# A recurrent attention and gated MLP kernel: the written order of its first part replaced on all engines

## The chip, the cores and the metric

The kernel runs on one core of one Trainium2 chip. The metric is the device time of one execution in microseconds (us); the time of a kernel is the median of its runs. A core has TensorE (PE; its weight loads are shown as PEld), VectorE (DVE), ScalarE (ACT), GpSimd (POOL) and SyncE (SP, which here only issues DMAs). Each engine works through its own queue in order and waits at semaphores for the others.

## The reference

A linear recurrence over 768 time steps for 4 batches and 8 heads of 48 channels, then a gated MLP over all 3072 tokens (model width 384, hidden width 1536). Everything is float32.

```python
for t in range(S):                                   # attention, per batch b and head h
    cur = einsum('bhd,bhe->bhde', u[None] * kt, vt)
    y[:, :, t] = einsum('bhd,bhde->bhe', rt, state + cur)
    state = w[None, :, :, None] * state + einsum('bhd,bhe->bhde', kt, vt)
...
gate = 1.0 / (1.0 + np.exp(-(x @ w_gate)))           # x: y as (tokens, 384)
val = x @ w_val
return (gate * val @ w_out).astype(np.float32)
```

## The kernel before

**The tiling.** Time is cut into 12 chunks of 64 steps, the heads into two halves; a chunk with a half is a *group*, and n counts the 24 groups (`GROUPS`, L34: half 1 of a chunk comes ahead of half 0). A group computes the 64x64 scores of keys and queries, applies them to the values, adds what the state gives, and updates the state. Two chunks (512 token columns, four groups) make one *tile* of x for the MLP; there are six. The MLP of a tile runs over 12 slices f of the hidden width, which the kernel calls items. Every operand of the MLP is split into a high part that the fast float32 mode holds exactly and a low rest, and a product is three passes (`PASS`, L499): 9 matmuls for the gate, 9 for the value (`up`, L507), 9 for the output (`down`, L546). x, the hidden activations and the weights are all split on the chip.

**What sets the order.** All engines run in the order in which the program is written (`manual_schedule`, L89). From tile 1 on, a loop (L674) writes it: gate and value of an item, at four items of the tile one group of attention, then the output of the item before. The first part, groups 0 to 7, all of tile 0 but its last `down`, and the first steps of groups 8 and 9, is written out by hand as a list of steps in `START` (L43), run by L650. It also holds all weight preparation. The change lies in this list and in the functions that its steps call.

**The steps**, with the engine that runs them (n is a group, f a weight slice; an item i of the old list stands for slice f and columns):
- SP: `L.n` loads queries and keys by channel (L100, tile `chan`, 3 buffers), `X.n` keys and values by token (L105, `toks`, 3 buffers), `Y.n` queries by token (L110), `W.f` one weight slice (L229, 1152 KB; f = 0 in two halves), `F.n` six DMAs that move parts of x between partitions (L480, L487).
- Preparing a group: `A.n` bonus keys (ACT, four instructions, L283), `R.n` queries (POOL; `Rv.n` on DVE, L291), `k.n` keys (DVE, L302), `T.n` token keys (POOL; `Tv.n` on DVE, L306).
- Attention on PE: `Z.n` scores (L366, two blocks of 32 small matmuls up to n = 7, into the one tile `sc`), `I.n` apply (L389, a block, and from n = 2 on a block more for the state, L347), `O.n` outer products (L407, a block). Behind them `K.n` copies the scores under masks (DVE, two instructions, L380), `d.n` decays the state (ACT, L424), `s.n` adds to it (DVE; `sa.n` on ACT, L435), `h.n` and `l.n` write the high and low part of x (ACT and DVE, L472, L476; two instructions, four for n = 1 and n = 3).
- A weight slice: `c.f` casts the upper words (ACT, L235), `j.f` joins the words (DVE, L242), `w.f` rounds to the high part (ACT, L251), `o.f` takes the low rest (POOL; `ov.f` on DVE, L257). A suffix 0 is a half of slice 0.
- The MLP: `U.i` gate and value (PE, 18 matmuls), `g.i` sigmoid (ACT, L522), `m.i` product (DVE, L527), `H.i` high part (ACT, L531), `q.i` low part (POOL; `qv.i` on DVE, L536), `D.i` output (PE, 9 matmuls). Items 0 and 1 are slices 0 and 1 on the first 256 columns (groups 0 and 1), items 2 and 3 the same slices on the other 256 (groups 2 and 3), items 4 to 13 slices 2 to 11 on all 512.
- Tables: `tc` constants, `tk`, `ti`, `tp`, `tr`, `tt`, `tn` powers of the decay in several layouts.

**PSUM.** `sc` takes two banks, `ring` (L71) has three banks, shared by the outputs of a group (two) and the gates and values of an item (one each), and `acc0` to `acc2` hold the output sums.

## Time and profile before

| | |
|---|---|
| median of 3 runs | 530.65 us (530.6 to 532.59) |
| span of the profiled execution | 532.9 us |
| PE busy | 510.4 us (96%) |
| PEld, DVE, ACT, POOL busy | 424.4, 203.4, 186.9, 189.9 us |
| DMA | 47.84 MB, mean 90 GB/s |

The span of the profiled execution lies 2.25 us over the median and inside 0.4 us of the slowest of the three runs. Busy time counts an engine's instructions without the semaphore and branch work between them; a matmul's end is modelled, so a busy PE need not be a PE at full pace. The pace of PE is read from the starts of matmuls of one shape.

### The profile page before, as it was taken

To read this page: it belongs to the slowest core of one execution; us is meant where nothing else is said; L and a number is where in the kernel's file an instruction comes from. 1 tells how busy PE (TensorE), PEld (TensorE's weight loads), DVE (VectorE), ACT (ScalarE), POOL (GpSimd) and SP (SyncE) were. 2 spreads that over 40 slices of the span, in tenths; PEclk is the share of its full clock that TensorE was granted. 3 is DMA by queue.
4 is the path that set the end of the run, shared out by engine and by line. 5 is a ranking of instruction groups with operands and counts; after the bars stand their busy time and mean duration, and the time that the engine had idled before them with its cause. 6 is when DMAs were issued, how large, how long until landed. Compare 5 with 4: busy or idle time off the path is not lost. (4 is left out here: it accounts for less than half of the span.)

```text
span 532.9 us, 11951 instructions
## 1 busy us (share of the span) xinstructions
PE 510.4 (96%) x5204; PEld 424.4 (80%) x5204; DVE 203.4 (38%) x344; ACT 186.9 (35%) x396; POOL 189.9 (36%) x159
## 2 busy tenths in 40 slices
...
GB/s 321 366 111 352 301 112 284 4 103 21 127 87 26 71 106 1 145 86 17 80 61 48 145 87 0 97 34 72 146 17 2 11 11 10 60 0 1 0 2 64
DMA packets 15723, 47.84 MB, mean 90 GB/s; under 512 B 2384, under 2 KB 5200, under 8 KB 14256
## 3 DMA queue, kind: packets, MB, share of 16 engines
...
q8 instruction: 43, 0.70, 0.6%
q14 instruction: 16, 0.13, 0.1%
...
## 5 line engine op out<-in xcount | busy, mean ns | idle before, releaser
L516 PE MATMUL ring<-xt,wx 128*128 128x512 f32 (+1 forms) x1332 | 309.9, 387 | 0.9 <-ACT sg L525 0.5
L516 PEld LDWEIGHTS ring<-xt,wx 128*128 128x128 f32 x1332 | 247.8, 191 | 51.3 <-ACT sg L525 0.7
L538 POOL TENSOR_TENSOR h<-sg,h 128x512 fp32r<-128x512 f32 (+1 forms) x66 | 88.5, 1340 | 259.5 <-ACT h L534 259.5
L554 PE MATMUL acc<-h,wx 128*128 128x512 f32 (+1 forms) x666 | 161.6, 388 | 0.4 <-POOLq L714 0.4
L554 PEld LDWEIGHTS acc<-h,wx 128*128 128x128 f32 x666 | 121.2, 188 | 25.6 <-POOLq L714 0.8
L529 DVE TENSOR_TENSOR sg<-ring,sg 128x512 f32<-128x512 f32 (+1 forms) x74 | 50.0, 676 | 237.0 <-PE ring L516 235.6
L525 ACT ACTIVATE sg<-ring 128x512 f32<-128x512 f32 (+1 forms) x74 | 43.4, 586 | 157.4 <-PE ring L516 157.4
L534 ACT CAST h<-sg 128x512 fp32r<-128x512 f32 (+1 forms) x74 | 45.0, 608 | 144.2 <-DVE sg L529 138.2
L293 POOL TENSOR_TENSOR dec<-chan,tabk 128x512 f32<-128x512 f32 x21 | 29.0, 1381 | 12.5 <-PE ring L337 12.4
L478 DVE TENSOR_TENSOR xt<-ring,xt 112x256 fp32r<-112x256 f32 (+1 forms) x52 | 19.9, 418 | 33.1 <-ACT xt L474 33.0
L308 POOL TENSOR_TENSOR toks<-toks,tabn 128x384 f32<-128x384 f32 x19 | 24.0, 1267 | 13.7 <-DMA toks<-in_tk 13.7
L314 POOL TENSOR_TENSOR dec<-dec,toks 128x384 f32<-128x384 f32 x16 | 16.3, 1020 | 27.3 <-DMA dec<-in_rt 27.3
L304 DVE TENSOR_TENSOR chan<-chan,tabk 128x512 f32<-128x512 f32 x24 | 25.0, 1042 | 0.9 <-ACT dec L287 0.9
L375 PE MATMUL sc<-dec,chan 48*64 48x64 f32 x768 | 17.4, 231 | 7.7 <-DVE chan L304 7.6
L383 DVE COPY_PREDICATED score<-masks,sc 128x512 f32<-128x512 int32 x32 | 23.9, 747 | 1.9 <-PE sc L375 1.1
L428 ACT ACTIVATE state<-state,pw 112x96 f32<-112x96 f32 x80 | 23.4, 362 | 2.6 <-PE ring L337 2.6
L337 PE MATMUL ring<-score,toks 64*48 64x64 f32 (+1 forms) x768 | 17.2, 230 | 5.0 <-DVE score L383 4.1
L447 DVE TENSOR_TENSOR state<-state,ring 48x192 f32<-48x192 f32 (+1 forms) x52 | 17.9, 350 | 9.7 <-ACT xt L474 4.7
L375 PEld LDWEIGHTS sc<-dec,chan 48*64 48x64 f32 x768 | 15.0, 145 | 8.1 <-POOL dec L293 7.6
L247 DVE SCALAR_TENSOR_TENSOR wf<-wr,top 128x1152 int32<-128x1152 int32 (+1 forms) x13 | 16.9, 1310 | 9.4 <-ACT top L240 5.7
L337 PEld LDWEIGHTS ring<-score,toks 64*48 64x48 f32 (+1 forms) x768 | 14.6, 137 | 6.4 <-DVE score L383 4.8
L474 ACT CAST xt<-ring 112x256 fp32r<-112x256 f32 (+1 forms) x52 | 16.7, 364 | 7.6 <-PE ring L337 7.3
...
## 6 DMA issues: line engine op xcount, KB each, us to landing
...
xt<-xt SPq DMA_DIRECT2D x12, 32.0 KB, 4.2
```

What stands on the lines that cost most here:

```text
L293: eng.tensor_tensor(v4(t[:, 0]), v4(chan[n][:, 0]), bc2(table_of(n)[:, :, ::-1]), ALU.mult)
L304: nc.vector.tensor_tensor(v4(k), v4(k), bc2(table_of(n)), ALU.mult)
L308: eng.tensor_tensor(v4(k), v4(k), bc2(tabn[:, 4 * g : 4 * g + 4]), ALU.mult)
L337: nc.tensor.matmul(yb[n][bank][64 * half : 64 * half + m, cs], lhsT, rhs, start=first, stop=stop, skip_group_check=True,)
L375: nc.tensor.matmul(sc[64 * gm : 64 * gm + 64, be, o : o + C], kk[row, cs : cs + C], rr[row, cs : cs + C], start=True, stop=True,)
L383: nc.vector.copy_predicated(t.rearrange("q (b m i) -> q b m i", b=2, m=4), masks[:, m].bitcast(I32).unsqueeze(1).unsqueeze(1).broadcast_to ...
L516: nc.tensor.matmul(o[:, self.cols], w[a][:, g * DM + kt * P : g * DM + (kt + 1) * P], self.x[:, kt, b, self.cols], start=(k == 0), stop=(k ...
L525: nc.scalar.activation(sg[:, c], self.pair[f][0][:, c], AF.Sigmoid, scale=UP)
L529: nc.vector.tensor_tensor(sg[:, c], self.pair.pop(f)[1][:, c], sg[:, c], ALU.mult)
L534: nc.scalar.copy(out=h[:, 0, c], in_=sg[:, c])
L538: eng.tensor_tensor(h[:, 1, c], self.sg.pop(f)[:, c], h[:, 0, c], ALU.subtract)
L554: nc.tensor.matmul(self.acc[d][:, self.cols], w[a][:, 2 * DM + d * P : 2 * DM + (d + 1) * P], h[:, b, self.cols], start=(f == 0 and k == 0 ...
```

## The change

- `START` is a new list. In the new one, loads go `L.0 X.0 L.1 W.0 L.2 L.3 X.1 W.1 X.2` (before: `L.0 W.0 L.1 X.0 W.1 L.2 X.1 X.2 W.2`), and the weight slices are used in the order 0, 1, 6, 7, 8, 4, 9, 10, 3, 5, 11, 2 for the gate.
- `U` is parted into `u` (gate, 9 matmuls) and `v` (value, 9 matmuls), each with a `ring` bank of its own taken when it is written. Items are named by slice, with a and b for the two column halves of slices 0 and 1.
- On PE the new list puts `Z.0` to `Z.3`, `I.0` to `I.2` and `O.0` to `O.2` ahead of the first gate; the old one had `Z.0` to `Z.2`, `I.0`, `I.1`, `O.0` and `O.1` there. 14 matmuls of the identity (`N.14`) stand ahead of `Z.0`.
- Other engines: seven `k` go from DVE to POOL (`kp`), two `A` from ACT to POOL (`Ap`), three `w` and two `h` from ACT to DVE (`wv`, `hv`), the order table from DVE to ACT (`trA`), one `s` to ACT; of the ten `R` five instead of three are on DVE, of the ten `T` one instead of three; fewer `o` and `q` are on DVE. The constants are cut into steps of their own.
- Group 1 writes its outputs to `acc1` and `acc2` instead of two `ring` banks.
- The loop from tile 1 on is the same; only the way in which it names items differs.

```diff
@@ -41,19 +41,20 @@
 
 
 START = """
-L.0 W.0 L.1 X.0 W.1 L.2 X.1 X.2 tc A.0 tk ti.1 R.0 ti.0 k.0 tp tr Z.0 tt K.0 I.0 c0.0 A.1 c0.1 tn
-h.0 c.1 T.2 T.1 k.1 Rv.1 j0.1 l.0 Tv.0 j0.0 Z.1 O.0 W.2 F.0 W.3 L.3 L.4 W.4 X.3 j.1 K.1 I.1 O.1 A.2
-w0.0 sa.0 w.1 h.1 w0.1 o0.1 o.1 R.3 Rv.2 k.2 o0v.0 l.1 s.1 Z.2 K.2 U.0 I.2 O.2 g.0 c.2 d.2 A.3 m.0
-U.1 H.0 g.1 h.2 j.2 k.3 s.2 l.2 q.0 T.3 m.1 F.2 L.5 W.8 X.4 L.6 W.5 W.6 L.7 X.5 F.1 X.6 L.8 W.7 Z.3
-K.3 I.3 O.3 w.2 A.4 k.4 H.1 c.3 h.3 l.3 R.4 D.0 Z.4 U.2 d.3 s.3 g.2 c.4 j.3 w.3 j.4 qv.1 m.2 o.2
-U.4 H.2 g.4 w.4 A.5 K.4 q.2 U.3 D.2 g.3 Rv.5 m.3 k.5 ov.3 m.4 T.4 I.4 O.4 Z.5 H.3 A.6 d.4 h.4 H.4
-c.6 c.5 k.6 s.4 K.5 l.4 Tv.5 j.6 R.6 q.3 D.1 D.3 U.5 I.5 g.5 h.5 j.5 qv.4 l.5 m.5 o.4 Z.6 D.4 R.7
-O.5 U.6 A.7 d.5 H.5 K.6 k.7 s.5 q.5 T.6 w.5 ov.5 U.7 c.8 c.7 g.6 j.7 m.6 L.9 X.8 ub Y.8 W.9 W.10
-X.7 I.6 Z.7 O.6 D.5 w.6 g.7 ov.6 d.6 w.7 H.6 s.6 j.8 qv.6 h.6 l.6 m.7 w.8 ov.7 H.7 qv.7 D.6 U.8 K.7
-R.8 c.9 ov.8 g.8 m.8 Tv.7 H.8 U.9 qv.8 g.9 k.8 j.9 w.9 o.9 m.9 D.7 U.10 g.10 H.9 c.10 j.10 m.10 q.9
-D.8 I.7 H.10 d.7 Z.8 O.7 h.7 w.10 D.9 s.7 U.11 ov.10 l.7 W.11 F.5 X.9 F.6 F.3 F.7 F.4 Y.9 qv.10
-g.11 c.11 j.11 D.10 U.12 m.11 w.11 R.9 ov.11 U.13 g.12 H.11 qv.11 m.12 H.12 qv.12 g.13 t.8 D.11 b.8
-i.8 D.12 K.8 k.9 m.13 H.13 q.13 b.9 T.9 t.9 i.9 T.8
+L.0 tov.0 ta tk tz ts.0 ts.1 ti.1 tc A.0 tp tb to.1 k.0 X.0 N.14 L.1 trA ti.0 R.0 A.1 Z.0 R.1 K.0
+W.0 tt I.0 tn Tv.0 c0.0 kp.1 L.2 L.3 c0.1 j0.0 X.1 Z.1 h.0 l.0 w0.0 A.2 O.0 K.1 I.1 R.2 k.2 W.1 X.2
+o0.0 Z.2 F.0 j0.1 T.1 R.3 A.3 h.1 kp.3 sa.0 w0.1 c.1 K.2 O.1 l.1 j.1 T.2 I.2 h.2 d.2 Z.3 w.1 O.2 l.2
+s.2 X.3 u.0a L.4 K.3 g.0a sa.1 W.6 o0.1 v.0a W.7 o.1 m.0a A.4 F.2 I.3 H.0a qv.0a Rv.4 kp.4 u.1a h.3
+D.0a l.3 g.1a c.6 T.3 L.5 v.1a Z.4 d.3 O.3 m.1a j.6 H.1a s.3 c.7 u.0b u.1b wv.6 v.1b A.5 g.0b v.0b
+W.9 qv.1a D.1a W.8 g.1b j.7 w.7 L.7 ov.6 c.8 m.1b m.0b H.1b o.7 u.6 q.1b u.7 H.0b K.4 g.6 j.8 qv.0b
+g.7 W.4 wv.8 v.7 c.4 X.4 ov.8 v.6 D.0b j.4 R.5 m.6 W.5 u.8 H.6 kp.5 D.1b q.6 m.7 T.4 w.4 H.7 W.11
+X.7 g.8 I.4 L.6 W.10 c.9 Z.5 ov.4 O.4 u.4 X.5 d.4 q.7 ub Rv.6 j.9 s.4 g.4 Ap.6 D.7 v.8 hv.4 l.4 K.5
+w.9 X.6 c.10 m.8 L.8 H.8 T.5 v.4 I.5 kp.6 Z.6 q.8 ov.9 Ap.7 d.5 m.4 O.5 u.9 W.3 j.10 D.8 s.5 hv.5
+w.10 c.3 l.5 K.6 j.3 kp.7 o.10 c.5 v.9 wv.3 W.2 u.10 j.5 H.4 c.2 g.9 Rv.7 D.6 qv.4 g.10 o.3 m.9 c.11
+j.11 H.9 v.10 m.10 w.5 T.6 ov.5 u.3 q.9 j.2 L.9 X.9 w.11 o.11 g.3 I.6 Z.7 d.6 O.6 s.6 T.7 u.5 h.6
+kp.8 D.4 l.6 H.10 Rv.8 qv.10 K.7 Y.8 v.3 m.3 g.5 u.11 I.7 Z.8 O.7 F.6 w.2 h.7 ov.2 d.7 l.7 X.8 F.7
+Y.9 Rv.9 D.9 k.9 s.7 D.10 u.2 H.3 q.3 g.2 v.5 b.8 v.2 m.5 b.9 H.5 D.3 i.8 T.9 i.9 m.2 H.2 T.8 qv.5
+t.8 t.9 g.11 v.11 m.11 D.5 K.8 q.2 H.11 D.2 q.11
 """
...
+    def bonus_keys_on(n, eng):
+        t, k, g = dec_of(n), chan[n][:, 1], GROUPS[n][1]
+        eng.tensor_tensor(
+            t[:, 1].rearrange("q (m x) -> q m x", m=4), k.rearrange("q (m x) -> q m x", m=4),
+            wu[:, 1, 4 * g : 4 * g + 4].unsqueeze(2).broadcast_to([P, 4, 2 * C]), ALU.mult,
+        )
...
     def outputs(n):
-        yb[n] = one_bank(), one_bank()
+        if n == 1:
+            yb[n] = tuple(pacc.tile([P, 512], F32, name=f"acc{i}") for i in (1, 2))
+        else:
+            yb[n] = one_bank(), one_bank()
...
+        def up_one(self, f, g):
+            w, o, k = (whi[f], wlo[f]), one_bank(), 0
+            self.pair.setdefault(f, []).append(o)
+            for kt in range(3):
+                for a, b in PASS:
+                    nc.tensor.matmul(
+                        o[:, self.cols], w[a][:, g * DM + kt * P : g * DM + (kt + 1) * P],
+                        self.x[:, kt, b, self.cols], start=(k == 0), stop=(k == 8),
+                    )
+                    k += 1
+
         def up(self, f):
...
+            self.up_one(f, 0)
+            self.up_one(f, 1)
...
     steps = {
+        "ta": identity, "tb": causal_masks, "tc": first_table,
+        "ts": clear_scores, "tz": lambda: clear_state(), "to": clear_top, "tov": lambda i: clear_top(i, V),
...
         "N": idle_matmuls,
+        "A": bonus_keys, "Ap": lambda n: bonus_keys_on(n, G),
+        "k": keys, "kp": lambda n: keys(n, G),
+        "h": x_high, "hv": lambda n: x_high(n, V.tensor_copy),
+        "wv": lambda f: round_weights(f, ALL, V.tensor_copy),
...
+    moe_steps = {
+        "U": Moe.up, "u": lambda m, f: m.up_one(f, 0), "v": lambda m, f: m.up_one(f, 1), "g": Moe.sigmoid, "m": Moe.product, "H": Moe.h_high, "q": Moe.h_low,
+        "qv": lambda m, f: m.h_low(f, nc.vector),
     }
...
-    for i in range(n0, len(items)):
+    for i in range(1, len(items)):
...
-        if i == n0 + 8:
+        if i == 9:
```

The function behind `N`, which both kernels have and only the new list calls:

```python
    def idle_matmuls(k):
        t = pacc.tile([P, 512], F32, name="acc2")
        for _ in range(k):
            nc.tensor.matmul(t[:, 0:P], ident, ident, start=True, stop=True)
```

## Rows read from the trace of the kernel before

**Rows 1.** The page, busy time of each engine over the whole span

```profile
PE 510.4 (96%) x5204; PEld 424.4 (80%) x5204; DVE 203.4 (38%) x344; ACT 186.9 (35%) x396; POOL 189.9 (36%) x159
```

**Rows 2.** Busy time by stage: stretch, length, busy us (instructions), granted clock, DMA share, GB/s

```profile
0.00:41.38 41.38, 26.91 (x690) 24.25 (x690) 30.68 (x55) 24.83 (x57) 19.57 (x26) 1.00 0.70 262
41.38:121.81 80.43, 79.23 (x938) 66.17 (x933) 54.69 (x76) 47.85 (x87) 22.80 (x15) 1.00 0.50 189
121.81:532.90 411.09, 404.30 (x3584) 333.97 (x3582) 118.07 (x214) 114.25 (x253) 147.53 (x119) 1.00 0.17 53
```

**Rows 3.** Waits of PE, 0 to 41.38 us: us in total, times, longest

```profile
PE sc L375 <- DVE chan L304: 7.6, 1, 7.6
PE ring L337 <- DVE score L383: 4.1, 3, 2.2
```

**Rows 4.** Longest wait of PE in 41.38 to 121.81 us, then behind 121.81 us

```profile
PE ring L337 <- issue: 0.3, 2, 0.2
...
PE acc L554 <- POOLq L714: 0.4, 1, 0.4
```

**Rows 5.** Timeline of PE in the first part: start us, busy us, instructions

```profile
7.63 1.13 PE L375 MATMUL sc<-dec,chan 48*64 48x64 f32 x32 [7.63 <-DVE chan L304]
...
24.18 3.78 PE L516 MATMUL ring<-xt,wx 128*128 128x256 f32 x16 [0.18 <-DVE xt L478]
...
33.89 1.33 PE L516 MATMUL ring<-xt,wx 128*128 128x256 f32 x9 [0.47 <-ACT sg L525]
35.15 0.69 PE L375 MATMUL sc<-dec,chan 48*64 48x64 f32 x32
35.67 0.65 PE L375 MATMUL sc<-chan,dec 48*64 48x64 f32 x32
...
41.38 8.89 PE L516 MATMUL ring<-xt,wx 128*128 128x256 f32 x54
...
121.81 4.24 PE L516 MATMUL ring<-xt,wx 128*128 128x512 f32 x18
```

**Rows 6.** DVE groups by form, 0 to 122 us: xcount | busy us, mean ns

```profile
L247 DVE SCALAR_TENSOR_TENSOR wf<-wr,top 128x1152 int32<-128x1152 int32 x11 | 15.4, 1411 | 9.4 <-ACT top L240 5.7 <-issue 3.5
L383 DVE COPY_PREDICATED score<-masks,sc 128x512 f32<-128x512 int32 x17 | 12.6, 744 | 1.4 <-PE sc L375 1.1
L304 DVE TENSOR_TENSOR chan<-chan,tabk 128x512 f32<-128x512 f32 x10 | 9.3, 927 | 0.9 <-ACT dec L287 0.9
L478 DVE TENSOR_TENSOR xt<-ring,xt 112x256 fp32r<-112x256 f32 x12 | 4.5, 414 | 0.0
L478 DVE TENSOR_TENSOR xt<-ring,xt 48x256 fp32r<-48x256 f32 x8 | 3.4, 422 | 2.7 <-ACT xt L474 2.6
L447 DVE TENSOR_TENSOR state<-state,ring 112x192 f32<-112x192 f32 x10 | 3.2, 349 | 9.1 <-ACT xt L474 4.7 <-PE ring L337 4.3
```

**Rows 7.** DVE timeline: the first low part of x

```profile
13.02 0.75 DVE L478 TENSOR_TENSOR xt<-ring,xt 112x256 fp32r<-112x256 f32 x2
```

**Rows 8.** POOL groups by form, 0 to 122 us, as in rows 6

```profile
L293 POOL TENSOR_TENSOR dec<-chan,tabk 128x512 f32<-128x512 f32 x7 | 11.0, 1566 | 12.5 <-PE ring L337 12.4
L258 POOL TENSOR_TENSOR wx<-wf,wx 128x1152 fp32r<-128x1152 f32 x4 | 10.7, 2672 | 16.0 <-ACT wx L255 16.0
L308 POOL TENSOR_TENSOR toks<-toks,tabn 128x384 f32<-128x384 f32 x5 | 6.2, 1247 | 13.7 <-DMA toks<-in_tk 13.7
```

**Rows 9.** POOL timeline: one and the same multiply, alone and beside a busy DVE

```profile
5.72 1.27 POOL L293 TENSOR_TENSOR dec<-chan,tabk 128x512 f32<-128x512 f32 x1
...
52.34 2.31 POOL L293 TENSOR_TENSOR dec<-chan,tabk 128x512 f32<-128x512 f32 x1
```

**Rows 10.** SP timeline: the six DMAs of F.0

```profile
13.79 4.40 SPq L482 DMA_DIRECT2D xt<-xt  x6
```

**Rows 11.** DMA issues, 0 to 75 us: KB each, median us from issue to landing

```profile
xt<-xt SPq DMA_DIRECT2D x12, 32.0 KB, 4.2
```

**Rows 12.** PE, the four transposes of 128x128 (L197)

```profile
L197 PE MATMUL acc<-spare,sg x4: 421/421/473, 9.5 to 10.2; 128*128 128x128 f32 x4
```

More of the change, by code (lines that the diff above doesn't have):

```diff
@@ L122, in rwkv_then_moe, with identity, causal_masks @@
     table = const.tile([P, 1], F32, name="table")
-    def constants():
+    def identity():
         make_identity(nc, ident)
+    def causal_masks():
         nc.gpsimd.memset(causal, 0.0)
@@ L133, in constants, with clear_scores, clear_state, first_table @@
             nc.gpsimd.tensor_copy(masks[lo : lo + 64, 1], ident[lo : lo + 64, lo : lo + 64])
-        for t in score:
-            nc.gpsimd.memset(t, 0.0)
-        nc.gpsimd.memset(state, 0.0)
+    def clear_scores(i, eng=nc.gpsimd):
+        eng.memset(score[i], 0.0)
+    def clear_state(eng=nc.gpsimd):
+        eng.memset(state, 0.0)
+    def first_table():
         nc.scalar.activation(table, ident[:, 0:1], AF.Sigmoid)
-        nc.vector.memset(tops[0].rearrange("q n two -> q (n two)").bitcast(F32), 0.0)
-        nc.gpsimd.memset(tops[1].rearrange("q n two -> q (n two)").bitcast(F32), 0.0)
+    def clear_top(i, eng=nc.gpsimd):
+        eng.memset(tops[i].rearrange("q n two -> q (n two)").bitcast(F32), 0.0)
     pw = const.tile([P, N2, 97], F32, name="pw")
@@ L300, in turn_queries, with keys @@
             nc.scalar.copy(out=turned(n)[to : to + 64], in_=src[:, :, 1])
-    def keys(n):
+    def keys(n, eng=nc.vector):
         k = chan[n][:, 1]
-        nc.vector.tensor_tensor(v4(k), v4(k), bc2(table_of(n)), ALU.mult)
+        eng.tensor_tensor(v4(k), v4(k), bc2(table_of(n)), ALU.mult)
     def token_keys(n, eng=nc.gpsimd):
@@ L470, in x_of, with x_high @@
         ]
-    def x_high(n):
+    def x_high(n, copy=nc.scalar.copy):
         for x, y in x_of(n, 0):
-            nc.scalar.copy(out=x, in_=y)
+            copy(out=x, in_=y)
     def x_low(n):
@@ L492, in fills @@
             for j in range(3) if g == 1 else ():
-                fill(xt[ti], j, slice(co, co + CT))
+                fill(xt[ti], j, slice(co, co + CT), eng)
         elif c == TILES[ti][-1]:
             for j in (2,) if g == 1 else (0, 1):
-                fill(xt[ti], j, slice(0, 2 * CT))
+                fill(xt[ti], j, slice(0, 2 * CT), eng)
     PASS = ((1, 0), (0, 0), (0, 1))
@@ L592, in store_last @@
             nc.sync.dma_start(out=out[2 * P : 3 * P, c + i], in_=o)
-    halves = [(0, g) for g in range(HALF)] + [(1, g) for g in range(HALF)] + [(2, g) for g in range(HALF, NF)]
-    items = [(0, h, f) for h, f in halves]
-    n0 = len(items)
+    items = [(0, 2, NF - 1)]
     for ti in range(1, len(TILES)):
@@ L609, in moe_of, with finish @@
         return moes[ti, h]
-    def finish(i):
-        ti, h, f = items[i]
-        moe_of(items[i]).down(f)
+    def finish(it):
+        ti, h, f = it
+        moe_of(it).down(f)
         if f == NF - 1:
```

72 lines of the change are left out of this document (35 added, 37 removed).

## The prediction

> **What bounds the kernel now.** I read the page first: PE is busy 96% of the span, every other engine under 40% [rows 1]. So the end is set by PE, and the change adds or removes no PE work that counts: 18 gate and value matmuls and 9 of output per slice remain, only written apart. What can move is the time in which PE waits or runs slowly. The second view is therefore busy time by stage, cut where it matters here. The first cut is at 41.38 us, the start of `U.2`, the first large block behind `Z.4`; the second at 121.81 us, where tile 1 begins and the unchanged loop takes over [rows 2, 5]. In the middle stage PE is busy 79.23 of 80.43 us and its longest wait is 0.3 us; in the loop the longest is 0.4 us [rows 2, 4]. There is nothing to win in either. In the first stage PE is busy only 26.91 of 41.38 us, and the waits are named: 7.6 us until the first keys are ready, 4.1 us for masked scores, the rest in smaller pieces [rows 2, 3].
>
> The third view, the timeline, shows a second loss. [...] Before 33.9 us, 16 matmuls of 128x256 take 3.78 us, 0.236 us each; from 33.89 to 35.15 us nine of the same take 1.26 us, 0.14 us each. A block of 32 score matmuls is busy 1.13 us at 7.63 us and 0.69 us at 35.15 us, and there the next begins 0.52 us later [rows 5]. [...]
>
> **The term that moves.** In the new order the same PE work stands ahead of `u.0b` as stood ahead of `U.2`: `Z.0` to `Z.4`, `I.0` to `I.3` with two state blocks, `O.0` to `O.3` (20 blocks), 36 half-width gate and value matmuls, 9 of output and the transposes. What follows up to tile 1 is the same too. So the question is when `u.0b` starts; call it M, 41.38 us now. At the upper pace the work ahead of it is 20 x 0.52 + 45 x 0.14 + about 0.7 = 17.4 us. Of the 24 us over that, 14.5 us are waiting and 9.5 us the lower pace.
>
> **The change, step by step, up to M.**
>
> *Start.* The first chain keeps its length: the channel load of group 0 is still first in SP's queue, the tables on DVE run in front of `k.0`, `R.0` is still behind the constants on POOL. `Z.0` stays at 7.6 us. Parting the constants and moving the order table to ACT lies beside this chain: ACT has nothing else to do between `A.0` and `A.1`. Group 1 writes to `acc1` and `acc2`, so the first gate needn't wait for its banks; `D.0a`, which takes them over, comes behind `l.1` and `sa.1` by several microseconds.
>
> *Idle matmuls.* Fourteen of 128x128. The nearest row is the four transposes: starts from 9.5 to 10.2 us, 0.22 us apart, 0.42 us for one alone [rows 12]. That makes 3.1 to 5.9 us behind the identity at about 1.4 us, so they end at 4.5 to 7.3 us, ahead of `Z.0`, and cost no time. What they give is unknown from this trace: nothing (PE stays at the lower pace until the gates come) up to the upper pace from `Z.0` on. I take the upper pace: PE's pauses in the chain below are all under two microseconds. If that is wrong, it is the first rival below.
>
> *To the first low part of x.* Now `l.0` ends at 13.77 us [rows 7], 6.1 us after `Z.0` begins. On the way lie three PE blocks; at the upper pace each ends 0.4 us sooner [rows 5]. So 12.6 us (13.8 at the lower pace).
>
> *From there DVE sets M.* In its new list stand, by the means of the rows: `K.1` 1.49, `k.2` 0.93, `j0.1` 0.71 (half of a full one), `K.2` 1.49, `l.1` 1.69 (four pieces), `j.1` 1.41, `l.2` 0.83, `s.2` 0.70, `K.3` 1.49, product and low part of 0a 0.84 (as two pieces of 256 columns), `Rv.4` 0.93, `l.3` 1.69, `m.1a` 0.42, `j.6` 1.41, `s.3` 0.70 [rows 6]. The sum is 16.7 us. The means include the slowing by POOL. Waits come on top: `K.2` for `Z.2`, which starts after `k.2` and takes 1.2 us, less `j0.1`: 0.5; `l.3` for `I.3` (1.2) and four casts on ACT (taken as long as the four subtractions, 1.7), less the 1.8 of work between: 1.1; `m.1a` and `s.3` for `v.1a` and `O.3`: 0.7. M = 12.6 + 16.7 + 2.3 = 31.6, rounded up to 32 us.
>
> *What lies beside it.* The six DMAs of `F.0` are issued from `l.0` on: 4.4 us to issue and 4.2 us to land [rows 10, 11], so the first gate can start at 21.2 us; from there PE needs 45 x 0.14 + 5 x 0.52 = 8.9 us, to 30.1: DVE is later. While SP waits for `l.0`, and later for `l.2` ahead of `F.2`, the loads written behind are held: `X.3` and `L.4` at first, then `L.5`, `W.9`, `W.8`. They are used at 26 us and later, 8 us after issue. POOL gets more: up to `o.1`, for which `u.1a` waits, it has five multiplies at 1.57, two token keys at 1.25, two half rests at 1.34 and one whole at 2.67 [rows 8], 15.7 us from about 8.3 us on, when `ti.0` is done: 24.0 us. `u.1a` is due at M less 27 x 0.14, three blocks and `s.3`, at 25.5 us: a margin of 1.5 us.
>
> **Behind M.** The stage takes 80.43 us now with 1.2 us of waiting. The load of the engines there changes as follows. DVE loses seven keys (6.5 us) and gains two multiplies and three roundings (between 0.9 and 1.5 us each; the trace has none on DVE, I take the 1.41 of a join of the same width); with the smaller moves it has about 6 us less over the whole first part. POOL gains seven multiplies in sum, two token keys and the rests and low parts, about 20 us on 42.4 [rows 2, 8], in 113 us. A parted `v` can wait for a PSUM bank that the sigmoid or product just before it must free, but the list puts an output block or another gate between. I allow another 1.2 us of PE waiting, because the lead that the others had on PE shrinks by what PE gains.
>
> **Sum.** 41.4 - 32 - 1.2 = 8.2 us less: the span goes from 532.9 to 524.7 us. The median is 2.25 us below the span of the profiled run, so 522.5 us.
>
> **Rivals.**
>
> *The lower pace stays.* If the idle matmuls don't lift the clock, or it falls back, `l.0` ends at 13.8, `F.0` lands at 22.4, and then PE itself sets M: 45 x 0.236 and five blocks of about 0.95 us make 15.4 us, to 37.8; if the pace rises on the way, as it did in the old run during such a stretch, about 36. The gain is 5.4 - 1.2 = 4.2 us: 526.5 us. For it: sparse blocks from 7.6 to 23 us did not raise the pace before.
>
> *POOL is late.* The same multiply took 1.27 us alone and 2.31 us beside a busy DVE [rows 9]. If all of POOL's 15.7 us stretch by 2.31 / 1.57, `o.1` ends at 31.4 us, `u.1a` starts there, and M is 31.4 + 6.2 = 37.6; less the later waits a gain of 2.6 us: 528 us. It decides from 1.5 us of stretch on. [...]
>
> *Slower: gates and values starve for banks.* Seven places of the new list (`v.0b`, `v.6`, `v.8`, `I.5`, `I.6`, `u.5`, `v.2`) take a bank that a sigmoid or product freed only one block earlier. If ACT or DVE is held there by a join, a rest or a rounding written in front (1.4 us each), PE stands. At 2 us a place that is 14 us, against 9.4 us won: 4.6 us slower, 535 us. It turns to a loss from 1.3 us a place. Against it: the old list, with the same three banks, lost 0.3 us at most in one wait [rows 4].
>
> *More than forecast.* If the waits on DVE vanish and its instructions run as when alone, M is near 28 us: 518.5 us.
>
> *No effect.* The order doesn't bind as I read it, and M stays: 530 us.
>
> **How the numbers follow.** Chances: forecast 0.45 (its own range 520 to 525 us), lower pace 0.24, POOL late 0.10, banks 0.09, more 0.07, no effect 0.05. The range 518.5 to 528.5 us takes in the first two, half of "more" and over half of "POOL late". Half a percent, 2.65 us, is about what a measurement of this kernel can tell from no change. Faster than 528.0 us: the first two, "more" and a part of POOL late, 0.78. Within: 0.13. Slower than 533.3 us: 0.09, nearly all from the banks.
>
> **What would show it.** Right: the first half-width gate of the second column half starts at 31 to 33 us, tile 1 at about 113 us, small blocks of 32 are busy 0.69 us from the first on, and PE waits little behind. Wrong: blocks of 1.13 us up to 25 us and more (lower pace); PE waiting for POOL's `wx` ahead of the gates of slice 1 (POOL late); waits of `ring` matmuls for `sg` of ACT or DVE spread from 40 to 110 us (banks); a start of tile 1 that has moved while the total has not, which would mean that the loop gives it back.

## The result, and the profile after

| | before | after |
|---|---|---|
| median, runs on one chip | 531.62 us (530.6 to 533.61) | 539.61 us (538.67 to 540.88) |
| span of the profiled execution | 532.9 us | 538.4 us |
| PE busy | 510.4 us | 515.0 us |
| DVE, ACT, POOL busy | 203.4, 186.9, 189.9 us | 209.4, 181.7, 215.4 us |

The ratio after to before is 1.0148, with a 95% interval of 1.012 to 1.0176. The change makes the kernel slower by 8 us. The forecast was 522.5 us, faster: wrong in sign and outside its range.

Busy time by stage of after, cut at the start of `u.0b` and of tile 1, with the columns of [rows 2]:

```profile
0.00:40.81 40.81, 29.93 (x717) 27.99 (x717) 28.30 (x46) 24.62 (x62) 23.09 (x29) 0.75 0.75 269
40.81:127.05 86.24, 80.81 (x935) 67.14 (x933) 63.92 (x78) 43.01 (x72) 49.41 (x29) 0.98 0.48 175
127.05:538.40 411.35, 404.30 (x3584) 333.98 (x3582) 117.18 (x212) 114.09 (x253) 142.89 (x115) 1.00 0.17 53
```

The loop is what it was (411.35 us against 411.09 in [rows 2]). `u.0b` starts at 40.81 us, 0.57 us earlier than `U.2` did, where 9.4 us were forecast. And the stage behind it, which should have grown by 1.2 us, grew by 5.81. PE's waits in the two first stages (us in total, times, longest us; the first five rows up to 40.81 us, the last three from there to 127.05 us):

```profile
PE sc L392 <- issue: 5.0, 2, 4.2
PE ring L351 <- DVE xt L495: 1.4, 1, 1.4
PE acc L640 <- POOL spare masks.py:199: 1.4, 1, 1.4
PE ring L351 <- DVE score L400: 1.2, 1, 1.2
PE acc L351 <- issue: 1.1, 1, 1.1
...
PE ring L351 <- issue: 3.0, 5, 2.4
PE ring L529 <- DVE xt L495: 1.0, 1, 1.0
PE ring L351 <- DVE sg L546: 0.9, 1, 0.9
```

The 4.1 us for masked scores of [rows 3] are down to 1.2, as meant. What is new carries the releaser "issue", which means that PE waited for nothing that the profile names: 4.2, 1.1 and 2.4 us in one piece. The timeline of PE shows where:

```profile
1.37 5.89 PE L640 MATMUL acc<-spare 128*128 128x128 f32 x28 [1.37 <-POOL spare masks.py:199]
8.07 0.69 PE L392 MATMUL sc<-dec,chan 48*64 48x64 f32 x32 [0.81 <-issue]
...
14.01 1.42 PE L351 MATMUL ring<-toks 64*64 64x48 f32 x32 [1.37 <-DVE xt L495]
...
18.40 1.24 PE L351 MATMUL acc<-toks 64*64 64x48 f32 x28
20.77 0.32 PE L351 MATMUL acc<-toks 64*48 64x48 f32 x2 [1.12 <-issue]
...
23.95 1.06 PE L392 MATMUL sc<-chan,dec 48*64 48x64 f32 x26
29.22 0.38 PE L392 MATMUL sc<-chan,dec 48*64 48x64 f32 x4 [4.21 <-issue]
...
30.45 3.95 PE L529 MATMUL ring<-xt,wx 128*128 128x256 f32 x18
...
55.69 2.23 PE L529 MATMUL ring<-xt,wx 128*128 128x512 f32 x9
...
61.21 0.52 PE L351 MATMUL ring<-toks 64*48 64x48 f32 x24
64.11 0.32 PE L351 MATMUL ring<-toks 64*64 64x48 f32 x8 [2.38 <-issue]
64.36 3.91 PE L529 MATMUL ring<-xt,wx 128*128 128x512 f32 x9
```

Each of the three pauses falls into the middle of a block of 32 matmuls whose operands are all there: behind 28 of `O.1`, behind 26 of the second block of `Z.3`, behind 24 of `O.4`. No wait is written at those places. From the first pause to the second PE runs, by the list, the last few of `O.1`, two blocks of `I.2`, one and most of a second of `Z.3`: some 126 matmuls, with as many weight loads 252 instructions. A number like it stands on the page, which counts DMA traffic that no instruction of the kernel issues:

```profile
PE 515.0 (96%) x5232; PEld 429.1 (80%) x5232; DVE 209.4 (39%) x335; ACT 181.7 (34%) x386; POOL 215.4 (40%) x172
...
q8 instruction: 43, 0.70, 0.5%
```

43 packets of 16 KB each (16,384 bytes, 0.70 MB in all). PE's 10,464 instructions in 43 packets are 243 to a packet. The reading that suggests itself: PE's own instructions come by DMA, and a pause is PE at the end of a packet with the next not there. The experiments below test it. The DMA queues of after say when the next came; the first row is the stretch from 18.5 to 26.4 us, the second from 26.5 to 27 us (packets that began there, MB, share of the 16 engines):

```profile
q1 hardware_dynamic: 498, 2.03, 79.6%
...
q8 instruction: 1, 0.02, 11.6%
```

Between 18.5 and 26.4 us no packet of instructions began. PE stopped at 25.0 us, the next packet began at 26.7 us and took 0.9 us, and PE went on at 29.22 us, 1.6 us behind its end. That last step is much the same everywhere. The traces of both kernels and of all runs below hold 33 waits of PE that are longer than 0.6 us, lie behind 10 us and have "issue" as their releaser. Each of them ends 1.2 to 1.6 us behind the end of an instruction packet. What filled the DMA engines ahead of the second pause is in SP's timeline (start, us of issuing):

```profile
14.32 3.96 SPq L499 DMA_DIRECT2D xt<-xt  x6
...
20.31 0.90 SPq L240 DMA_DIRECT2D wr<-in_wt  x2
```

The six DMAs of `F.0`, then `X.3` and `L.4`, and right ahead of the pause `W.6` and `W.7`, two loads of 1152 KB. In the 4 us ahead of the packets that ended the three pauses, of 1.12, 4.21 and 2.38 us, the DMA share was 0.91, 0.97 and 0.97. In the loop it is 0.17, and PE's longest wait there is 0.4 us.

The granted clock of after, in the same columns as above, for three stretches. The column counts time without a clock record as 1.00; the first record of after stands at 6.6 us, at 1.00:

```profile
0.00:13.48 13.48, 9.26 (x192) 8.66 (x192) 11.04 (x18) 7.76 (x18) 9.95 (x20) 1.00 0.85 308
13.48:33.98 20.50, 14.07 (x336) 13.24 (x337) 11.51 (x20) 10.95 (x29) 10.72 (x7) 0.50 0.70 252
...
64.85:68.05 3.20, 3.20 (x9) 2.48 (x8) 3.05 (x8) 0.00 (x0) 1.75 (x2) 0.50 0.78 267
```

With the idle matmuls ahead of it `Z.0` is busy 0.69 us, the upper pace, where [rows 5] had 1.13, the lower. The granted clock fell to 0.50 at 13.5 us, in PE's wait from 12.64 to 14.01 us ahead of `O.0`, and rose to 1.00 at 34.0 us, when PE had worked since 29.22 us with no pause. Behind the third pause it fell to 0.50 once more, and the nine matmuls at 64.36 us took 3.91 us, where nine of the same took 2.23 at 55.69 us: that pause cost 2.4 + 1.7 us.

The last new piece is DVE beside POOL. First the timeline of DVE, queries (L307) and joins (L254), then that of POOL, two rests (L265):

```profile
84.92 3.16 DVE L307 TENSOR_TENSOR dec<-chan,tabk 128x512 f32<-128x512 f32 x1
...
91.70 1.36 DVE L254 SCALAR_TENSOR_TENSOR wf<-wr,top 128x1152 int32<-128x1152 int32 x1 [1.60 <-issue]
...
95.45 3.69 DVE L254 SCALAR_TENSOR_TENSOR wf<-wr,top 128x1152 int32<-128x1152 int32 x1
...
102.04 0.68 DVE L307 TENSOR_TENSOR dec<-chan,tabk 128x512 f32<-128x512 f32 x1
```

```profile
83.87 3.66 POOL L265 TENSOR_TENSOR wx<-wf,wx 128x1152 fp32r<-128x1152 f32 x1 [2.15 <-issue]
...
94.32 3.60 POOL L265 TENSOR_TENSOR wx<-wf,wx 128x1152 fp32r<-128x1152 f32 x1
```

Beside a rest the queries took 3.16 us and the join 3.69; without one they took 0.68 and 1.36. The two ended 0.6 and 1.2 us behind the end of the rest beside them, nearly the time that each takes without one. The rests took 3.66 and 3.60 us, where [rows 8] have 2.67 in the mean. PE waited 0.5, 0.9 and 1.0 us for DVE, up to 90, 94 and 102 us.

### The profile page after: what moved, and what is told of

The parts are those of the page before. It is cut to its first block, busy times and chain, and to the rows that moved or that the text cites. A ratio compares the mean times of both kernels' runs of the same rounds, so it can differ in the third digit from the quotient of the medians.

```text
span 538.4 us, 12012 instructions
## 1 busy us (share of the span) xinstructions
PE 515.0 (96%) x5232; PEld 429.1 (80%) x5232; DVE 209.4 (39%) x335; ACT 181.7 (34%) x386; POOL 215.4 (40%) x172
## 5 line engine op out<-in xcount | busy, mean ns | idle before, releaser
L555 POOL TENSOR_TENSOR h<-sg,h 128x512 fp32r<-128x512 f32 (+1 forms) x68 | 94.1, 1384 | 264.1 <-ACT h L551 264.1
L322 POOL TENSOR_TENSOR toks<-toks,tabn 128x384 f32<-128x384 f32 x21 | 29.0, 1384 | 0.0
L307 POOL TENSOR_TENSOR dec<-chan,tabk 128x512 f32<-128x512 f32 x19 | 25.1, 1320 | 2.2 <-DVE tabk L185 1.8
L265 POOL TENSOR_TENSOR wx<-wf,wx 128x1152 fp32r<-128x1152 f32 (+1 forms) x7 | 18.1, 2582 | 15.7 <-ACT wx L262 13.4
L254 DVE SCALAR_TENSOR_TENSOR wf<-wr,top 128x1152 int32<-128x1152 int32 (+1 forms) x13 | 22.6, 1739 | 2.3 <-issue 1.6
L351 PEld LDWEIGHTS ring<-dec,state 48*64 48x64 f32 (+1 forms) x448 | 12.6, 137 | 8.0 <-issue 6.7
L247 ACT ACTIVATE top<-wr 128x1152 f16<-128x1152 bf16 (+1 forms) x13 | 18.3, 1430 | 1.5 <-DMA wr<-in_wt 0.8
L351 PE MATMUL ring<-toks 64*64 64x48 f32 (+1 forms) x672 | 15.1, 220 | 3.7 <-issue 2.4
L318 DVE TENSOR_TENSOR chan<-chan,tabk 128x512 f32<-128x512 f32 x17 | 18.4, 1080 | 0.0
L351 PE MATMUL ring<-score,toks 64*48 64x64 f32 (+1 forms) x736 | 15.6, 223 | 2.3 <-DVE score L400 1.2
## 6 DMA issues: line engine op xcount, KB each, us to landing
wr<-in_wt SPq DMA_DIRECT2D x11, 1152.0 KB, 10.1
```

The source lines that it names most:

```text
L254: nc.vector.scalar_tensor_tensor(w32[f].bitcast(I32)[:, c], middle, 13, t, ALU.logical_shift_right, ALU.bitwise_or)
L307: eng.tensor_tensor(v4(t[:, 0]), v4(chan[n][:, 0]), bc2(table_of(n)[:, :, ::-1]), ALU.mult)
L322: eng.tensor_tensor(v4(k), v4(k), bc2(tabn[:, 4 * g : 4 * g + 4]), ALU.mult)
L351: nc.tensor.matmul(yb[n][bank][64 * half : 64 * half + m, cs], lhsT, rhs, start=first, stop=stop, skip_group_check=True,)
L555: eng.tensor_tensor(h[:, 1, c], self.sg.pop(f)[:, c], h[:, 0, c], ALU.subtract)
```

## The experiments

The theory: PE runs out of instructions, because the new list packs small matmuls more densely and puts loads of data in front of PE's packets. Its rivals: the lower pace of PE sets the time, and the pauses only fall into slack; or the shares given to POOL and DVE are the loss.

**Where the pause stands.** e1 is after without the idle matmuls, e2 with 10 for 14 (each of them shows as two matmuls on PE: 28 and 20), e5 with `u.0a`, nine matmuls, ahead of `Z.3`. The edits of `START` in that order, cut to the words around them:

```diff
-k.0 X.0 N.14 L.1 trA
+k.0 X.0 L.1 trA
...
-k.0 X.0 N.14 L.1 trA
+k.0 X.0 N.10 L.1 trA
...
-I.2 h.2 d.2 Z.3 w.1 O.2 l.2 s.2 X.3 u.0a L.4
+I.2 h.2 d.2 u.0a Z.3 w.1 O.2 l.2 s.2 X.3 L.4
```

> The new kernel without its 14 idle matmuls. Its trace has pauses of PE in the middle of a block, released by nothing the profile shows: after 26 of the 32 matmuls of the second block of Z.3 for 4.21 us, after 28 of 32 of O.1 for 1.12 us, after 24 of 32 of O.4 for 2.38 us. Theory 1 (PE runs out of instructions, which come in packets of the queue of kind instruction): the idle matmuls are 28 matmuls with 28 weight loads in the profile, so without them each pause comes 28 matmuls later in the list: the one of Z.3 moves into O.2, after 22 of 32. Theory 2 (a wait of the program that the profile doesn't name): they stay where they are. For the time: if the upper pace from 8 to 13 us was worth something, this run is 1 to 3 us slower than the new kernel; if the pauses are what counts and they get shorter because PE uses up its instructions more slowly, it is the same or up to 3 us faster.

> The new kernel with 10 idle matmuls instead of 14: 8 matmuls and 8 weight loads fewer in the profile ahead of Z.0. Theory 1 (PE runs out of instructions at fixed counts of its list): the pause in Z.3 after 26 of 32 comes 8 matmuls later, after 2 of the 32 of O.2. Theory 2 (a wait of the program): it stays after 26 of 32 of Z.3. The time should be that of the new kernel within 2 us by both.

> The new kernel with the first gate, u.0a (9 matmuls of 128x256), moved from behind O.2 to between I.2 and Z.3, so that the run of small matmuls from Z.2 to O.2 is broken by a block that takes longer per instruction. Pauses of PE come every 126 to 127 matmuls of its list (counts 221, 348, 474 from the first idle matmul on). Theory 1 (a packet of instructions is asked for when the one before it begins to be used, so a pause is the packet's delay less the time that PE needs for the 126 matmuls between): the pause at count 474 now falls into the second block of Z.3 after 17 of 32, and it shrinks from 4.21 us by the time of u.0a at the lower pace, about 2 us. The second column half, u.0b, starts 1 to 2 us earlier than 40.8 us and the kernel gets 1 to 2 us faster. Rival (F.0 or the low part of x isn't there yet at 21 us): u.0a waits instead, the pause moves into that wait, and the time stays within 1 us.

e1 took 538.22 us, ratio 1.0113 (1.0086 to 1.0139); e2, one execution, 541.14 us; e5 538.87 us, 1.0126 (1.0096 to 1.0155). PE's timeline around the pause, of e1, e2 and e5:

```profile
25.86 0.85 PE L351 MATMUL ring<-toks 64*64 64x48 f32 x22
29.63 0.55 PE L351 MATMUL ring<-toks 64*48 64x48 f32 x10 [2.92 <-issue]
```

```profile
23.92 0.39 PE L351 MATMUL ring<-toks 64*64 64x48 f32 x2
27.77 1.08 PE L351 MATMUL ring<-toks 64*64 64x48 f32 x30 [3.46 <-issue]
```

```profile
23.40 0.41 PE L392 MATMUL sc<-chan,dec 48*64 48x64 f32 x16
27.39 0.71 PE L392 MATMUL sc<-chan,dec 48*64 48x64 f32 x16 [3.58 <-issue]
```

28 matmuls fewer ahead of it move the second pause 28 matmuls on (the last 6 of `Z.3` and 22 of `O.2`); 8 fewer move it 8 on; 9 more move it from 26 to 16 (17 was expected). It stands where the count of PE's instructions puts it, whatever the block is and whatever data it reads. The third pause moves by 8 in e2 as well, to the end of `O.4`. Not every end of a packet shows a pause: the first is gone in e2 and e5; in e1 the first and the third are gone, and pauses of 1.36 us (behind 25 of `I.1`) and 2.29 us (at 92.5 us) stand at other packet ends.

The length does not follow from the count: in e5 I expected about 2 us and got 3.58; when a packet is asked for, no run shows. Nor does the start of `u.0b` alone set the time. It came at 37.38 us in e5 and at 38.82 in e2, 3.4 and 2.0 us earlier than in after, and tile 1 still began at 126.47 and 126.98 us, against 127.05. In e5 a wait of 1.41 us for ACT's sigmoid at 50 us is part of what took it back.

e1 also weighs the idle matmuls: with them gone all blocks up to 30 us ran at the lower pace (scores busy 1.08 to 1.13 us), `u.0b` began at 41.05 us against 40.81, and the kernel is not slower. So in after the upper pace wins nothing that can be measured. Whether the 28 matmuls cost anything isn't shown: the median of e1 is 1.4 us under that of after, but the two intervals overlap, and further down e13, which is e10 without them, has the ratio of e10 within 0.0005.

**What makes it long.** e3 writes `W.6` and `W.7` behind `F.2` on SP; e8 has ACT issue them behind `w.1` (`Wa`), and puts `W.11` and `X.7` behind `W.2`, away from the third pause.

```diff
-u.0a L.4 K.3 g.0a sa.1 W.6 o0.1 v.0a W.7 o.1 m.0a A.4 F.2 I.3
+u.0a L.4 K.3 g.0a sa.1 o0.1 v.0a o.1 m.0a A.4 F.2 W.6 W.7 I.3
...
-d.2 Z.3 w.1 O.2
+d.2 Z.3 w.1 Wa.6 Wa.7 O.2
-u.0a L.4 K.3 g.0a sa.1 W.6 o0.1 v.0a W.7 o.1 m.0a A.4 F.2 I.3
+u.0a L.4 K.3 g.0a sa.1 o0.1 v.0a o.1 m.0a A.4 F.2 I.3
-w.4 H.7 W.11 X.7 g.8
+w.4 H.7 g.8
-wv.3 W.2 u.10
+wv.3 W.2 W.11 X.7 u.10
```

> The new kernel with the loads W.6 and W.7 (1152 KB each) written behind F.2 instead of ahead of it. In the new kernel they were issued at 20.3 to 21.2 us, and the instruction packet that ended the 4.21 us pause of PE came at 26.6 us. Theory 1a (the packet is late because these loads fill the DMA engines): the pause in Z.3 stays at the same place but shrinks to under 1.5 us, the first gate comes about 3 us earlier, and the kernel gets 2 to 4 us faster. Theory 1b (the packet is late by itself): the pause stays at 4 us and the time the same. Theory 3 (DVE sets the start of u.0b anyway): the pause shrinks, but the time stays within 1 us.

> The new kernel with four loads moved away from the two long pauses of PE and nothing held up behind them. W.6 and W.7 are issued by ACT behind w.1 (about 26 us) instead of by SP at 20.3 us, so that F.2 no longer stands behind them nor they behind F.2; W.11 and X.7, used only from 90 us on, are issued behind W.2 instead of at 45 us. Theory 1a (the instruction packets are late because data loads fill the DMA engines): the pause of Z.3 (4.21 us) falls to under 1.5 us, that of O.4 (2.38 us) to under 1.5 us; with the lower pace that follows each pause, u.0b starts near 37 us, tile 1 at 122 to 124 us, and the kernel gets 3 to 5 us faster than the new one, to the time of the one before. Theory 1b (packets are late by themselves): pauses as before and the time within 1 us of the new kernel. Theory 3 (DVE sets the start of u.0b): pauses shrink, the time doesn't.

In e3 the second pause fell from 4.21 to 1.74 us (under 1.5 was expected) and the first gate began at 27.42 us instead of 30.45, though the first and third grew to 2.27 and 2.96 us. But the kernel took 542.85 us, ratio 1.0199 (1.017 to 1.0228), where 2 to 4 us less were expected: `W.6` came late, ACT's cast of it waited 3.81 us, the join `j.6` on DVE waited for that, and PE waited for `s.3`, which stands behind `j.6`. The timeline of PE in e3:

```profile
42.34 4.88 PE L529 MATMUL ring<-xt,wx 128*128 128x256 f32 x27 [2.83 <-DVE state L464]
```

e8 has both at once, shorter pauses and the weights in time: 536.01 us, ratio 1.0072 (1.0044 to 1.01). That takes back half of the loss, and the interval lies clear of that of after. `u.0b` starts at 37.44 us, and these are the second and third pause on its timeline of PE, the third above the 1.5 us that were expected:

```profile
25.22 0.38 PE L392 MATMUL sc<-chan,dec 48*64 48x64 f32 x4 [1.19 <-issue]
...
60.22 0.32 PE L351 MATMUL ring<-toks 64*64 64x48 f32 x8 [1.88 <-issue]
```

The same instructions, the same place: 4.21 us with the loads in front, 1.19 without. One trace each would be thin, since the first pause alone runs from under 0.6 to 2.27 us in traces that have the same instructions ahead of it. But the other runs agree. The second pause took 2.92 to 4.21 us in the five traces with `W.6` and `W.7` in front (after, e1, e2, e5, e6) and 1.19 to 1.74 us in the three without (e3, e8, e9); with the gate ahead of `Z.3` as well, e5 has 3.58 us and e10, with the loads moved, none. The third took 2.38 to 2.96 us in the five traces that have it with `W.11` and `X.7` in front (after, e2, e3, e5, e6) and 0.64 to 1.88 us in the five that have it without (e8 to e11, e14). So these loads lengthen the two pauses. For the first pause no run moved the loads.

**Parts of the change in the old kernel.** e4 is before with the idle matmuls, e7 before with the first loads in the new order.

```diff
-ti.0 k.0 tp tr Z.0
+ti.0 k.0 tp tr N.14 Z.0
...
-L.0 W.0 L.1 X.0 W.1 L.2 X.1 X.2 tc
+L.0 X.0 L.1 W.0 L.2 X.1 W.1 X.2 tc
```

> The kernel before with the 14 idle matmuls ahead of Z.0 and nothing else of the change. The clock theory (in the old kernel 9.5 us of the first 41 are lost to the lower pace, and the idle matmuls raise it from 8 us on): the granted clock is 1.00 from 7 us on, with blocks of 0.69 us, and if it holds the kernel gets 2 to 5 us faster. If it falls again in the pauses of PE behind Z.1 (2.2 us there in the old trace), as it fell at 13.4 us in the new kernel, less than 1 us is won. Theory 1 adds: the list of PE is shifted by 56 instructions, so a pause of 1 to 4 us inside a block of small matmuls may appear that the old kernel hadn't; then it is up to 4 us slower.

> The kernel before with only the order of its first loads like that of the new one: L.0 X.0 L.1 W.0 L.2 X.1 W.1 X.2 instead of L.0 W.0 L.1 X.0 W.1 L.2 X.1 X.2. Theory 5 (the loads were the part of the change that could win): X.1 and L.1 land 2 to 3 us sooner, the waits of PE for masked scores and token keys up to 21 us (4.1 and 1.7 us) shrink by 1 to 3 us in sum, and the kernel gets 1 to 2 us faster, unless an instruction packet that now comes later takes it back. Rival (the joins of slice 0 and 1 in front of K.1 and l.0 on DVE wait for the weights that now land later): the wait moves to DVE and the time is the same or up to 2 us worse.

e4 took 532.56 us, ratio 1.0017 (1.0 to 1.0034): the clock fell to 0.50 at 13.8 us (a mean of 0.67 from 13 to 34 us), `U.2` began at 39.02 us, and a pause of 1.27 us stands at 60.6 us that before hasn't. e7 took 532.53 us, 1.0024 (1.0005 to 1.0043): PE's longest wait for masked scores grew to 4.71 us. Neither part makes the old kernel faster, and neither is the 8 us.

**The shares of DVE and POOL.** e6 is after with the rests `o.3` and `o.11` on DVE; e9 is e8 with that; e10 is e9 with e5's gate ahead of `Z.3`.

```diff
-g.10 o.3 m.9
+g.10 ov.3 m.9
...
-w.11 o.11 g.3
+w.11 ov.11 g.3
```

> The new kernel with the low rests of slices 3 and 11 on DVE instead of POOL. In the new kernel these two ran from 83.9 to 87.5 us (3.66 us) and from 94.3 to 97.9 us (3.60 us) on POOL, against 2.69 us alone, while beside them on DVE a multiply took 3.16 us (0.68 alone) and a join 3.69 us (1.36 alone); behind these PE waited 0.5, 0.9 and 1.0 us for DVE at 90, 93 and 101 us. Theory 4 (POOL and DVE slow each other, and this is 2.4 us of the loss behind u.0b): the two DVE instructions fall to under 1.5 us each, DVE has 2.7 us more work but 4 to 5 us less of stretch, and the three waits of PE shrink to under 0.8 us in sum; the kernel gets 1.5 to 2.5 us faster. Rival (DVE is simply late in this stretch by its amount of work): the waits stay or grow and the time is the same or up to 2 us worse.

> The kernel with the four loads moved (W.6 and W.7 to ACT, W.11 and X.7 later) and with the low rests of slices 3 and 11 on DVE as well. The rests alone gave some 2 us. If the losses by the pauses and by POOL and DVE slowing each other add up, this is 5 to 7 us faster than the new kernel and 0 to 2 us faster than the one before; if they hide each other, it is as the run with the loads alone, within 1 us.

> As the one before it in this set, with u.0a ahead of Z.3 in addition, which alone moved the start of u.0b from 40.8 to 37.4 us and left the time as it was, since PE then waited for ACT and for weights at 50 us. If those waits came from loads that were late, then with the loads moved this is another 1 to 2 us faster (to 527 to 530 us); if the middle of the first part is bound by the arrival of weights 6, 7 and 4, it is the same within 1 us, and PE waits at 45 to 55 us for ACT's sigmoids, which stand behind the casts.

e6: 537.4 us, ratio 1.0122 (1.0088 to 1.0156), an interval that overlaps that of after. In its trace the queries took 0.68 us instead of 3.16 and the join 2.05 instead of 3.69. PE's waits of 0.9 and 0.5 us for DVE's products are gone; the one for the low part of x, 1.0 us in after, is 1.1. e9: 534.88 us, 1.0039 (1.001 to 1.0068). e10: 533.76 us, 1.0038 (1.0013 to 1.0064), with `u.0b` at 36.95 us and its longest pause 0.99 us. From after to e8 to e9 the ratio falls from 1.0148 by 0.0076 and by 0.0033, where the intervals of e8 and e9 overlap; the gate adds nothing that can be measured.

**Is it the pace after all?** e11 adds 18 idle matmuls to e10, in PE's waits ahead of `I.0`, `O.0` and `I.1`.

```diff
-W.0 tt I.0 tn
+W.0 tt N.2 I.0 tn
...
-A.2 O.0 K.1 I.1 R.2
+A.2 N.4 O.0 K.1 N.3 I.1 R.2
```

> The kernel with loads moved, rests on DVE and u.0a early, with 9 more idle matmuls in the places where PE waits before 16 us: 2 ahead of I.0, 4 ahead of O.0, 3 ahead of I.1. In the new kernel the granted clock fell from 1.00 to 0.50 at 13.4 us, in the wait ahead of O.0, and stayed there until 34 us. Clock theory (the fall comes from these waits, and the lower pace of the blocks behind is part of what keeps u.0b from the 32 us that were forecast): the granted clock stays at 1.00 up to 20 us at least, blocks are busy 0.69 us, u.0b starts 1 to 3 us earlier than the 36.95 us of the run without them and the kernel gets 1 to 2 us faster. Rival (at the upper pace the 126 matmuls between two packets of instructions are done sooner, so PE only waits longer for the packet): the blocks are quicker, the pauses near 20 and 25 us longer by as much, and u.0b and the time stay within 1 us.

534.68 us, ratio 1.0052 (1.0028 to 1.0077). The granted clock now stayed at 1.00 up to about 20 us and blocks were busy 0.66 to 0.69 us, where e10 has 1.10 to 1.26 from 15 to 18 us. `u.0b` began at 36.69 us against 36.95 in e10, and the time is no less. PE reached the end of its packet sooner and stood there longer, 1.57 us instead of 0.99, and waited 0.75 us for DVE's scores at 30 us, where e10 has 0.74 (timeline of PE in e11):

```profile
16.43 0.66 PE L392 MATMUL sc<-chan,dec 48*64 48x64 f32 x32
...
19.70 0.49 PE L351 MATMUL acc<-toks 64*64 64x48 f32 x22 [1.57 <-issue]
...
36.69 4.58 PE L529 MATMUL ring<-xt,wx 128*128 128x256 f32 x36
```

So up to 20 us the lower pace is not what sets the time: the faster PE waited longer for its instructions, and as long for DVE at 30 us. Behind the third pause of after it does cost, as the 1.7 us above show.

**The old kernel again**, unchanged, one execution, 533.37 us:

> The kernel before once more, unchanged, for a second trace of it. The trace that the prediction rests on is of an execution of 532.9 us span; if the device time is some 1.8 us above the span, as in the runs of the new kernel, that execution was among the slowest of the old kernel. Expected, if so: a span of 529 to 531 us and U.2 at 39 to 40.5 us instead of 41.4 us; if that trace was typical: 41 us or later again.

Its busy time by stage, cut at the starts of `U.2` and of tile 1:

```profile
0.00:39.53 39.53, 24.79 (x690) 22.31 (x690) 31.88 (x55) 25.34 (x58) 19.62 (x26) 0.87 0.74 274
39.53:118.73 79.20, 78.55 (x939) 65.97 (x934) 53.92 (x76) 47.30 (x85) 21.38 (x15) 1.00 0.52 193
118.73:531.60 412.87, 404.30 (x3584) 333.96 (x3582) 117.36 (x214) 114.10 (x253) 147.47 (x119) 0.99 0.17 53
```

The span is 531.6 us, a little over the 529 to 531 expected. `U.2` began at 39.53 us instead of 41.38 and tile 1 at 118.73 instead of 121.81: the execution on which the prediction rests was a long one. The granted clock is at 1.00 for good from 28.5 us on here and from 33.2 us on there. Against this one, after reaches tile 1 8.3 us later, about the difference of the medians (8.0 us). The old kernel has a pause too, 1.24 us up to 19.6 us in this trace.

**The last 0.4%.** e13 is e10 without the idle matmuls, e14 e10 with `ov.11` behind `l.6` and `j.2` behind `K.7` instead of ahead of `s.6`, e15 both.

```diff
-q.9 j.2 L.9 X.9 w.11 ov.11 g.3 I.6
+q.9 L.9 X.9 w.11 g.3 I.6
...
-kp.8 D.4 l.6 H.10 Rv.8 qv.10 K.7 Y.8
+kp.8 D.4 l.6 ov.11 H.10 Rv.8 qv.10 K.7 j.2 Y.8
```

> e10 without the 14 idle matmuls on PE ahead of O.1 (28 instructions in PE's stream). If what is left of the loss (e10 stands at 1.0038 of the kernel before) lies in where PE's packets of instructions run out, the pauses move by 28 matmuls as they did from the changed kernel to e1, and the time falls by 1 to 2 us against e10, to a ratio of about 1.001. If the pauses stand wherever they stand and cost the same, the ratio stays at 1.003 to 1.005.

> e10 with the join ov.11 on VectorE behind l.6 and j.2 behind K.7, where e10 has both ahead of s.6. If VectorE's work ahead of s.6 and l.6 is what makes PE wait 1.1 us for VectorE at about 93 us, that wait is gone and the time falls by about 1 us, to a ratio of about 1.002. If the wait only moves to what reads j.2 or ov.11, or to the stretched work beside GpSimd, the ratio stays at 1.003 to 1.005.

> Both edits on e10: no idle matmuls, and ov.11 and j.2 later on VectorE. If both causes hold and add, some 2 to 3 us less than e10: a ratio of 0.998 to 1.000, the first version that isn't slower than the kernel before. If neither does, 1.003 to 1.005.

532.88, 533.92 and 533.44 us; ratios 1.0033 (1.0001 to 1.0064), 1.005 (1.0027 to 1.0073) and 1.0038 (1.0017 to 1.006). PE's wait of 1.1 us at 93 us is gone in e14 and e15, and the time is not less. Without the idle matmuls (e13, e15) one pause of 1.36 us at 17 us stands for e10's three of 0.99, 0.86 and 0.64, and the time is about the same. In all three runs it was the second of the two outcomes that was named, no gain; the intervals are too wide to rule out 1 us.

One hint is left on the rest. The traced executions of e10 and e15 (531.64 and 531.66 us; tile 1 at 118.55 and 118.58 us) reach tile 1 as early as the old kernel does above, but each is the shortest of its ten: the medians are 2.1 and 1.8 us higher. The traced execution of e14 took 534.74 us, with the same PE instructions as e10 up to 60 us; its pauses are 0.86, 1.41 and 1.88 us. And the one of e9, at 537.59 us, has a wait of 2.42 us for token keys from a DMA and pauses of 1.03, 1.74 and 1.37. So pauses at the same place of nearly the same list differ by up to 1.2 us from one execution to the next (0.64 us in e10 and 1.88 in e14, at 60 us). Whether the new list suffers more from that than the old one isn't shown: the ten runs of e15 spread from 531.66 to 535.5 us, and 25 of the old kernel beside them from 530.01 to 535.05. No version that was run beats the kernel before.

## Why the prediction was wrong, point by point

- **What bounds the kernel: right.** PE sets the end, the loop didn't move, and all of the difference lies ahead of tile 1.
- **The path to M, "from there DVE sets M", with PE's share put at its work: the step that failed.** The prediction lets the first gate start at 21.2 us, when `F.0` has landed, gives PE 8.9 us from there, and finds DVE later. "At the upper pace the work ahead of it is 17.4 us", and the rest is waits for other engines or the lower pace: the supply of PE's own instructions is put at nothing, with no reason given. Measured, the first gate began at 30.45 us, behind pauses of 1.12 and 4.21 us, and from 29.22 us to `u.0b` at 40.81 us PE waited 0.2 us in all. So it was PE's own row of work behind the second pause that set M. 126 small matmuls take, by an estimate, some 1.9 us at the upper pace and 3.4 at the lower (from blocks of 32, which start 0.48 and 0.85 to 0.86 us apart); the next packet began 1.7 us after PE had stopped, and PE went on 2.5 us after that. No row of [rows 1 to 12] has a packet, and the prediction didn't read the line of the page that counts them. Why the old list has fewer such pauses is only argued: its waits for scores and keys [rows 3] may hide them.
- **`l.0` ends at 12.6 us: 14.29.** The new list puts `Tv.0` and `j0.0` ahead of `l.0` on DVE, where the old one has them behind it; they took 1.00 and 1.85 us, and `l.0` began when they ended. The working passed over that.
- **DVE's list of 16.7 us: near in size, its waits mis-sized.** The terms far off are the half join `j0.1`, 1.55 us and not 0.71, the low part of 0a, 1.03 and not 0.42, and `Rv.4`, 1.50 and not 0.93. DVE was busy 16.44 us from 14.29 to 40.81 us and had not ended `j.6` when `u.0b` began; `s.3` came at 41.44 us. Its waits were 10.1 us, not 2.3, and 6.3 of these are the single wait for `O.2` behind PE's pause.
- **The idle matmuls: they did what was hoped, and it was worth nothing.** They ended at 7.3 us, the upper of the two bounds, and `Z.0` ran at the upper pace, which held up to 13.5 us. That it holds through pauses under two microseconds was the author's assumption, and no run shows it: in after the clock fell in a wait of 1.37 us. They are 28 matmuls with 28 weight loads in PE's stream, costed at nothing because they lie ahead of `Z.0`, and move the end of every packet by 28 matmuls; what that costs isn't shown (e1, e13).
- **Behind M 1.2 us: it was 5.8.** The pause at 61.7 us (2.4), the lower pace behind it (1.7) and PE's waits for DVE (2.4) are 6.5 us, some of it in place of the 1.2 us that PE waited in the old stage.
- **"Lower pace stays": it happened, but its price was not what it said.** The granted clock was at 0.50 from 13.5 to 34.0 us. e1, with the lower pace from the start, and e11, with the upper up to 20 us, moved M by 0.2 to 0.3 us and the time by nothing that can be measured.
- **The pace read from the trace of before: right.** The 1.00 that [rows 2] have for the first stretch is no record against it: that trace has no clock record ahead of 33.2 us, and the column counts such time as 1.00. Its first record, at 1.00, stands at 33.2 us, just ahead of where [rows 5] have the matmuls get quick. Record and pace agree.
- **"POOL late", "banks": neither decided.** `o.1` was in time. POOL's work takes longer beside DVE's, as the first has it, only later, and DVE's takes longer too: a rest on POOL took 3.66 us instead of 2.67, on DVE the queries 3.16 instead of 0.68 and a join 3.69 instead of 1.36. e9 against e8 puts what it costs PE at 0.0033 of the time, 1.8 us. PE waited for DVE's `sg` at two places, 1.4 us in all, not at seven.
- **The median 2.25 us below the span: wrong.** In each execution of the record with both numbers the time is 1.7 to 1.9 us above the span (540.11 to 538.4, 533.37 to 531.6). By that the traced execution of before took some 534.7 us, an estimate, 3 us over the median, so its 41.38 us for `U.2` promised a gain that the median didn't have to give: with 39.5 us the same working gives 7.5 instead of 9.4 us ahead of M. That is luck of the trace, and too small to turn the sign.

**Shown and only argued.** That the pauses stand at the ends of PE's packets is shown (e1, e2, e5, and the packets' own times), and that the loads ahead of the second and third lengthen them (e3, e8 and the traces beside them). That moving these four loads takes back half of the loss is shown by e8. The 1.8 us for DVE and POOL side by side rest on two kernels whose intervals overlap, so the size is rough. What makes the first pause, why a packet is late by just so much, and the last 0.3 to 0.5%, stay open.
